# Loading beta in its final layout behind a weight load, and reordering two groups of casts, in an attention + MoE kernel

## The chip, the cores and the metric

The kernel runs on one core of one Trainium2 chip. The metric is device time in microseconds (us); a number given for a kernel is the median of its runs unless said otherwise. A profiled execution has in addition a span, which is about 1.7 us shorter than the time of the same execution (before: 283.81 us and 282.1 us). Names of engines: PE does matrix multiplies (its weight loads are listed apart as PEld), DVE is the vector engine, ACT the scalar engine, POOL is GpSimd, SP issues DMAs.

## The reference, cut to what matters

```python
# q, k, v: 8 batches x 8 heads x 576 x 64
q_s = exp(q - max) / sum            # softmax over the head dimension
k_s = exp(k - max) / sum            # softmax over the sequence
kv  = einsum("bhsd,bhse->bhde", k_s, v)
x   = einsum("bhsd,bhde->bhse", q_s, kv)      # -> 4608 tokens x 512
h   = x @ w_in                                # 512 x 2048
g   = h * (1 / (1 + exp(-beta * h)))          # beta: 2048 values
out = g @ w_out                               # 2048 x 512
```

## The kernel before

The parts that the change touches. `beta` (2048 floats) is loaded as four rows of 512, transposed on PE by four small matmuls, and multiplied by 0.5 into `beta_h`, which is the scale of every tanh.

```python
nc.gpsimd.dma_start(beta_r[:], moe_beta.rearrange("(b n) -> b n", b=4))
...
for blk in range(1, 4):                 # 512 columns of w_in each
    load_w_in(blk, 0, 2)                # SP; two rows of k-tiles per load
    load_w_in(blk, 2, 4)
for j0 in range(0, NJ, 2):
    load_w_out(j0)
make_identity(nc, ident[:])
make_identity(nc, identf[:])
...
dummy(4, CH)                            # warm-up matmuls
...
bt = bank("A1", [P, 4, 4], F32, "bt")
for i in range(4):
    nc.tensor.transpose(bt[:, i], beta_r[:, i:CH:4], identf[:])
dummy(1, CH)
...
nc.vector.tensor_scalar(beta_h[:], bt[:].rearrange("p i b -> p b i"), 0.5, None, op0=ALU.mult)
...
nc.scalar.activation(th[:], h[:], ACTF.Tanh, scale=beta_h[:, i // 4, i % 4 : i % 4 + 1])
```

Batch 0 is prepared at the head. While PE runs the MoE part of the first tokens, the loads of w_in, w_out and of batch 1's q, k and v arrive, and batch 1 is prepared in the same way (exp on ACT, sums and divisions on DVE, transposes and small matmuls on PE). From then on PE runs nearly without a gap.

The softmax here doesn't subtract the row's maximum and nothing guards it: scores larger than these inputs give would overflow.

## Time and profile before

| | before |
|---|---|
| time, median of 3 runs | 283.27 us (283.04 to 283.30) |
| span of the profiled run | 282.1 us |
| PE busy | 97% of the span |
| landing of q of batch 1, first half: median engine, last engine | 34.77 us, 36.88 us |
| first weight load of the dense part | 47.58 us |
| last weight load minus first of the dense part | 231.12 us |

"Landing" is read from the trace's completion records: each load has sixteen, one for each DMA engine, and an instruction that waits for the load waits for the last of them. The views of the profile that bound the time are shown in the prediction below. In the page's table of DMA queues of the kernel before (packets, MB, share of sixteen engines' span), these are the queues that bring instructions to the engines:

```profile
q8 instruction: 13, 0.21, 0.3%
q14 instruction: 10, 0.08, 0.1%
```

The trace has 16,384 bytes for each packet of the first and 8,192 for each of the second. And in the chain that ended last (start, length, what), the last piece is ACT's copy of the last output:

```profile
279.06 0.28 ACT o L532
```

The span ends at 282.07, so 3.01 us pass from the start of that copy to the end: the copy, the store, its landing, and the closing barrier.

### The profile page before, as it was taken

The numbers are of one execution on the slowest core, as the hardware profiler recorded it, in microseconds if no ns is written. First come the engines' busy times: TensorE is split into PE (matmuls) and PEld (weight loads), VectorE is DVE, ScalarE is ACT, GpSimd is POOL, SyncE is SP. The second block draws the span as 40 slices with busy tenths as digits, with TensorE's granted clock in tenths as the row PEclk, the third lists the DMA queues.
The fourth block names the chain that finished last, engine by engine and source line by source line (L and its number), as shares of the span: only waits on it lengthen the run. The fifth ranks groups of instructions, "written<-read, shape, count | busy, mean of one in ns | idle before, by whom it ended". The sixth has DMA issues, their size and how long they took to land.

```text
span 282.1 us, 4611 instructions
## 1 busy us (share of the span) xinstructions
PE 273.7 (97%) x1664; PEld 136.2 (48%) x1692; DVE 155.5 (55%) x282; ACT 168.1 (60%) x280; POOL 70.5 (25%) x120
## 2 busy tenths in 40 slices
PE   7989999999999999999999999999999999999995
PEld 3545445545444445444444444444444444444444
DVE  2947359976865485638564766466453333444401
ACT  4856367867965587457854785478454544444411
POOL 3368831450631054104510361027000000000000
PEclk9999999999999999999999999999999999999999
DMA  7999999889799908991699069904200200031112
GB/s 242 371 392 406 388 385 359 291 141 359 176 202 354 209 37 183 326 230 64 141 315 285 34 143 305 279 32 110 79 37 2 76 37 37 2 76 37 40 74 74
DMA packets 51559, 51.69 MB, mean 183 GB/s; under 512 B 21068, under 2 KB 41932, under 8 KB 51536
## 3 DMA queue, kind: packets, MB, share of 16 engines
q1 hardware_dynamic: 51360, 51.33, 60.9%
q8 instruction: 13, 0.21, 0.3%
q14 instruction: 10, 0.08, 0.1%
q10 hardware_dynamic: 144, 0.07, 0.1%
q0 software_dynamic: 32, 0.01, 0.0%
HBM read 38.28 MB, written 9.44 MB: 169 GB/s over the span
## 4 chain that ended last, share of the span: by engine, by line
PE 83%; DMA 13%; ACT 1%; issue 1%; SPq 1%; ACTq 0%
PE acc L509 40%; PE h L457 39%; DMA k<-in_k_dram 7%; DMA wo<-in_moe_w_out_dram 3%; DMA wi<-in_moe_w_in_dram 3%; PE kv L384 2%; PE x L408 2%; PE kv L259 0%; ACT Ek L230 0%; SPq L105 0%; ACT o L538 0%; SPq L117 0%; PE xt L422 0%; PE tp L217 0%; ACT va L152 0%
## 5 line engine op out<-in xcount | busy, mean ns | idle before, releaser
L471 DVE SCALAR_TENSOR_TENSOR g<-th,h 128x512 bf16<-128x512 bf16 x144 | 97.3, 685 | 98.5 <-ACT th L469 98.2
L469 ACT ACTIVATE th<-h,beta_h 128x512 bf16<-128x512 f32 x144 | 97.1, 689 | 85.7 <-PE h L457 82.7
L509 PE MATMUL acc<-w_out_b,g 128*128 128x512 bf16 (+2 forms) x590 | 142.8, 368 | 1.7 <-issue 1.1
L457 PE MATMUL h<-xT,w_in_b 128*128 128x512 bf16 x503 | 127.6, 379 | 1.0 <-POOL w_in_b L161 0.4
L457 PEld LDWEIGHTS <-w_in_b 128*128 128x128 bf16 x576 | 64.8, 113 | 61.9 <-POOL w_in_b L161 1.4
L509 PEld LDWEIGHTS <-g 128*128 128x128 bf16 x608 | 56.9, 98 | 63.9 <-issue 2.5
L315 POOL TENSOR_TENSOR Eq<-Eq,qz 128x512 bf16<-128x512 bf16 x24 | 25.1, 1049 | 84.3 <-issue 41.0
L538 ACT ACTIVATE o<-acc 128x512 f32<-128x512 f32 x34 | 20.0, 591 | 8.9 <-PE acc L509 7.4
L161 POOL TENSOR_SCALAR_AFFINE_SELECT va<-v 128x256 bf16<-128x256 f32 (+3 forms) x55 | 21.6, 427 | 13.8 <-DMA v<-in_v_dram 13.5
L355 ACT ACTIVATE Ek<-k 128x640 bf16<-128x640 f32 x24 | 17.7, 737 | 0.0
L457 PE MATMUL h<-xTt,w_in_b 128*128 128x512 bf16 x63 | 16.4, 379 | 0.1
L313 DVE TENSOR_REDUCE qz<-Eq 128x8 f32<-128x512 bf16 x24 | 16.2, 675 | 0.0
L305 ACT ACTIVATE Eq<-q 128x512 bf16<-128x512 f32 x24 | 14.7, 623 | 0.0
L201 DVE TENSOR_REDUCE qz<-Eq 128x16 f32<-128x1024 bf16 x4 | 4.9, 1216 | 10.8 <-ACT Eq L194 10.8
L166 DVE CAST xT<-x 128x512 bf16<-128x512 f32 x15 | 10.3, 685 | 0.6 <-PE x L408 0.5
L582 PE MATMUL warm<-zf 128*128 128x512 f32 (+1 forms) x14 | 9.0, 778 | 1.5 <-DVE zf L549 1.5
L161 POOL TENSOR_SCALAR_AFFINE_SELECT w_in_b<-wi 128x512 bf16<-128x512 f32 x16 | 9.5, 612 | 3.9 <-DMA wi<-in_moe_w_in_dram 3.8
L152 ACT CAST xT<-x 128x512 bf16<-128x512 f32 x17 | 9.7, 578 | 0.8 <-PE x L408 0.7
L194 ACT ACTIVATE Eq<-q 128x1024 bf16<-128x1024 f32 x4 | 4.2, 1056 | 9.5 <-DMA q<-in_q_dram 9.5
L341 POOL TENSOR_TENSOR Et<-Et,zt 128x512 bf16<-128x512 bf16 x4 | 4.2, 1042 | 21.0 <-DVE zt L340 21.0
L161 POOL TENSOR_SCALAR_AFFINE_SELECT w_out_b<-wo 128x1024 bf16<-128x1024 f32 x8 | 8.3, 1039 | 1.9 <-DMA wo<-in_moe_w_out_dram 1.8
L408 PE MATMUL x<-qT,kvn 64*64 64x512 bf16 x64 | 6.0, 391 | 0.4 <-ACT xT L152 0.4
(52 smaller groups left out, 78.3 us busy)
## 6 DMA issues: line engine op xcount, KB each, us to landing
q<-in_q_dram SPq DMA_DIRECT2D x16, 512.0 KB, 6.2
out_dram<-o SPq DMA_DIRECT2D x31, 256.0 KB, 3.1
k<-in_k_dram SPq DMA_DIRECT2D x24, 320.0 KB, 7.5
v<-in_v_dram SPq DMA_DIRECT2D x24, 320.0 KB, 7.5
wo<-in_moe_w_out_dram SPq DMA_DIRECT2D x8, 512.0 KB, 10.4
wi<-in_moe_w_in_dram SPq DMA_DIRECT2D x6, 512.0 KB, 9.7
k<-in_k_dram SPq DMA_DIRECT2D x4, 576.0 KB, 8.8
v<-in_v_dram SPq DMA_DIRECT2D x6, 288.0 KB, 8.6
```

The lines of the kernel that those rows point to most:

```text
L161: nc.gpsimd.affine_select(out=dst, in_=src, pattern=[[0, n]], base=0, channel_multiplier=0, compare_op=ALU.is_equal, fill=fill0,)
L166: eng.tensor_copy(dst, src)
L305: nc.scalar.activation(by_pair(Eq[b], m).rearrange("p t h d -> p h t d"), ld["q", b, hf][:, a : a + 2, :].rearrange("p h (t d) -> p h t d" ...
L313: nc.vector.tensor_reduce(z, e, axis=AX.X, op=ALU.add)
L315: nc.gpsimd.tensor_tensor(e, e, z.unsqueeze(3).to_broadcast((P, NT, 2, D)), ALU.mult)
L355: nc.scalar.activation(Ek[b][:, :, h0:h1, :].rearrange("p t h d -> p h t d"), ld["k", b, hf][:, a : a + h1 - h0, :].rearrange("p h (t d) - ...
L408: nc.tensor.matmul(xps[b, 2 * g + c][o, :], kvn[b][r, j, :], qT[b][r, g, a] if b < EARLY else qT[b][r, :, j, :], start=True, stop=True,)
L457: nc.tensor.matmul(hs[n, i][:], w_in_b[:, kt, blk * CH + r : (blk + 1) * CH : 4], rhs_a(n, kt), start=(kt == 0), stop=(kt == KT - 1),)
L469: nc.scalar.activation(th[:], h[:], ACTF.Tanh, scale=beta_h[:, i // 4, i % 4 : i % 4 + 1])
L471: nc.vector.scalar_tensor_tensor(out=g[:], in0=th[:], scalar=1.0, in1=h[:], op0=ALU.add, op1=ALU.mult)
L509: nc.tensor.matmul(acc[n, st][:, c0:c1], gs[n, j][:, min(st, 3) * P : (min(st, 3) + 1) * P], w_out_b[:, j, c0:c1], start=(j == 0), stop=(j ...
L538: nc.scalar.activation(o[:], acc[n, st][:], ACTF.Copy, scale=0.5)
```

## The change

The intent is to take beta's four transposes off PE and its copy off the path at the head, to have beta early enough for the first tanh all the same, and to take two places out where PE waited for a cast: w_in's second block (its second half now cast on POOL and DVE at once) and batch 1's v (ACT's part moved ahead).

```diff
@@ tiles
-    identf = const.tile([4, 4], F32, name="identf")
-    beta_r = const.tile([4, CH], F32, name="beta_r")
+    beta_p = const.tile([P, 4, 4], F32, name="beta_p")
@@ loads
-    nc.gpsimd.dma_start(beta_r[:], moe_beta.rearrange("(b n) -> b n", b=4))
     for blk in range(1, 4):
         load_w_in(blk, 0, 2)
+        if blk == 1:
+            nc.sync.dma_start(beta_p[:], moe_beta.rearrange("(b p i) -> p b i", b=4, i=4))
         load_w_in(blk, 2, 4)
     make_identity(nc, ident[:])
-    make_identity(nc, identf[:])
@@ head
-    bt = bank("A1", [P, 4, 4], F32, "bt")
-    for i in range(4):
-        nc.tensor.transpose(bt[:, i], beta_r[:, i:CH:4], identf[:])
-    nc.vector.tensor_scalar(
-        beta_h[:], bt[:].rearrange("p i b -> p b i"), 0.5, None, op0=ALU.mult
-    )
@@ behind x_out(0, 3)
+    nc.vector.tensor_scalar(beta_h[:], beta_p[:], 0.5, None, op0=ALU.mult)
@@ casts of w_in
-            cast_w_in(blk, k0, nc.gpsimd)
+            if (blk, k0) == (1, 2):
+                t, _ = ld["wi", 1, 2]
+                cast(nc.gpsimd, w_in_b[:, 2, CH : 2 * CH], t[:, 0])
+                cast(nc.vector, w_in_b[:, 3, CH : 2 * CH], t[:, 1])
+            else:
+                cast_w_in(blk, k0, nc.gpsimd)
@@ batch 1 (b_mm(n): n matmuls of the second MoE product put in between)
-        b_mm(20)
+        b_mm(6)
+        ev_cast(1, 0, 1, nc.scalar, 0, 4)
+        b_mm(14)
         ...
-        ev_cast(1, 0, 1, nc.scalar, 0, 4)
         ...
-        b_mm(1)
+        b_mm(2)
         ...
-        b_mm(4)
+        b_mm(3)
```

## The prediction

> **What bounds the kernel now.** I read the page first (PE busy 97% of a span of 282.1 us, so every microsecond gained or lost has to show as PE starting its dense part earlier or later), then the table by stage, then the chain of waits and the timeline of the first 48 us, because every line that the change touches runs there. The table by stage, with columns for length, PE, PEld, DVE, ACT and POOL busy time with counts, clock, DMA share and GB/s:
>
> ```profile
> 0.00:15.03 15.03, 12.74 (x96) 6.64 (x98) 8.63 (x20) 9.93 (x17) 5.43 (x19) 1.00 0.88 312
> 15.03:29.39 14.36, 13.92 (x62) 7.05 (x63) 8.81 (x15) 8.80 (x15) 10.54 (x17) 1.00 1.04 400
> 29.39:40.90 11.51, 11.34 (x52) 4.99 (x52) 4.95 (x8) 4.44 (x7) 6.02 (x7) 1.00 1.05 385
> 40.90:47.60 6.70, 6.32 (x72) 3.27 (x74) 6.03 (x15) 5.33 (x13) 1.95 (x4) 1.00 1.08 362
> 47.60:282.00 234.40, 229.36 (x1387) 114.25 (x1408) 127.04 (x228) 139.60 (x231) 46.61 (x76) 1.00 0.54 147
> ```
>
> The last stage, 234.4 us, is nearly pure matmul and the change does not touch it: its length is a constant, and the end moves by as much as its start, 47.6 us, moves. Up to 40 us the DMA engines are never idle (share 1.04, 1.05: saturated), and the chain of waits of that window says the same:
>
> ```profile
> 2.91 7.96 DMA k<-in_k_dram
> 10.89 8.77 DMA wi<-in_moe_w_in_dram
> 19.72 9.26 DMA wo<-in_moe_w_out_dram
> 28.99 10.90 DMA k<-in_k_dram
> 39.91 1.26 ACT Ek L230 x2
> ```
>
> The reader sees start and length: four loads cover 36.9 of the first 39.9 us. What then sets 47.6 is in the timeline of batch 1:
>
> ```profile
> 36.90 1.06 ACT L194 ACTIVATE Eq<-q 128x1024 bf16<-128x1024 f32 x1 [6.18 <-DMA q<-in_q_dram]
> 37.99 1.22 DVE L201 TENSOR_REDUCE qz<-Eq 128x16 f32<-128x1024 bf16 x1 [6.49 <-ACT Eq L194]
> ...
> 42.48 0.52 PEld L259 LDWEIGHTS <-Ek 64*128 64x128 bf16 x18 [0.82 <-ACT va L152]
> ...
> 43.49 0.45 PEld L217 LDWEIGHTS <-Eq 128*128 128x128 bf16 x8 [0.28 <-DVE Eq L205]
> ...
> 44.91 0.10 PEld L408 LDWEIGHTS <-kvn 64*64 64x64 bf16 x1 [0.43 <-DVE qT L166]
> 45.23 0.11 PEld L408 LDWEIGHTS <-kvn 64*64 64x64 bf16 x3 [0.22 <-ACT kvn L279]
> ...
> 47.16 0.20 PEld L408 LDWEIGHTS <-kvn 64*64 64x64 bf16 x4 [0.42 <-DVE kvn L281]
> ```
>
> ACT sat 6.18 us until q of batch 1 landed at 36.88. From there DVE works with hardly a gap (6.03 of 6.70 us in the stage): exp 1.06, reduce 1.22, reciprocal 0.25, multiply 1.23 end at 40.76, the second half's three end at 43.43, and PE's transposes at 40.91 and 43.49 start just behind them. The x matmuls at 45.23 wait for kvn on ACT, behind Ek at 42.92, which waits for k landing at 42.89. So four of the five waits shown hang on the landing of q or k of batch 1, and only the one at 42.48 on the order of the casts. From 36.88 to the first matmul of the dense part (47.58) I count 10.7 us of fixed chain.
>
> The completion records of the trace (sixteen for each load, one per DMA engine) show why these landings are late. The load of w_in block 1's second half lands on fifteen engines by 17.86 and on the sixteenth at 19.66; every later load keeps that gap (q of batch 1: 35.29 against 36.88). At 16.87 a 16,384-byte instruction packet of 1,095 ns went through one engine. One straggling engine sets the landing times.
>
> **What the Trainium skill says.** (1) "DMA: Bandwidth & Descriptors", section Specifications: below 512 bytes per descriptor a transfer does not reach line rate (a read-modify-write). The trace agrees: the loads of the q tails, 512 pieces of 256 bytes or 32 per engine, take 0.67 to 0.86 us between consecutive landings, 21 to 27 ns a piece, where 2,048 bytes take 84 ns. (2) Same page, "Issuing engines are not separate DMA queues": loads from POOL and SP share the same 16 engines. So moving beta to SP wins no bandwidth and puts it in line with the others. (3) "SBUF — State Buffer", section "Who interferes with whom": a DVE cast or tensor_scalar in a 2-port mode and a GpSimd instruction block each other for a whole instruction. The trace fits: DVE L289 took 0.50 us beside POOL's casts at 23.91 and 0.23 us at 53.25. (4) "Advanced Engine Details and Errata", ISA Cache: instructions come in lines of 16 KB, 256 instructions. The trace has 13 such packets; the first starts when PE has executed 217 instructions.
>
> **The change part by part.**
>
> Removed: the four transposes of beta. On PE they are 7.60 to 8.17:
>
> ```profile
> L597 PE MATMUL bt<-identf,beta_r 4*128 4x4 f32 x4 | 0.6, 262 | 0.0
> ```
>
> 0.57 us of PE time at the head. I give 0 of it to the end: the matmuls that follow wait elsewhere. kv of group 1 (12.39) follows POOL's cast of v, which follows v landing at 11.62; ACT's chain follows k landing at 10.87; x and then h at 15.03 follow these. DVE loses the beta_h multiply of 0.17 us at 12.12, but its next path instruction waits for kv anyway. POOL's identf (0.09 + 0.18 us) and beta's software DMA (0.70 us) go in front of an idle time of 5.9 us: 0.
>
> Added: one load of 512 pieces of 16 bytes, 32 per engine, on the saturated queue in front of w_in block 1's second half. Four-byte semaphore packets take 9 ns, 256-byte pieces 21 to 27 ns, most of it fixed (256 bytes at 2,048 bytes in 84 ns are 10.5 ns, so 11 to 16 ns are overhead). I estimate 9 to 16 ns for 16 bytes: 32 x 9 to 16 = 0.29 to 0.51 us, mid 0.4, on every engine including the straggler. Beta's old load, 2 KB on each of four engines, saves at most 0.08 us there. So every landing from w_in block 1's second half to v of batch 1 comes **0.35 us later**.
>
> Moved, cast of w_in: before, POOL cast k=2 and k=3 in turn from 19.72, and PE's first two matmuls on them ran at 20.39 and 20.95 where back-to-back spacing of 0.216 us would have had 20.21 and 20.43. With the landing at 20.0, if POOL and DVE overlap, both are cast by 20.7, and the second matmul starts at about 20.97: the move gains 0.34 and the landing takes 0.35, so PE comes out even. If they lock each other out (a DVE cast of some 0.35 to 0.6 us), PE comes out 0.3 later. DVE's own multiplies g wait behind that cast: g of unit 0 starts at about 20.4 instead of 18.54; at 0.62 us each, the eighth ends at about 25.9, just when PE wants its bank for unit 12. All this is before 29.39; PE then runs 52 matmuls and arrives at the transpose of batch 1 at 40.8 to 41.1, where Eq is not there before 40.76 + 0.35. So it is hidden either way.
>
> Beta's landing: 17.1 to 17.3 by my count (the load before it ends at 16.76 + 0.4), the multiply 0.17, and the first tanh needed it at 17.82: no wait, unless the instruction packet falls just on it. With eight PE instructions fewer ahead of it, that packet moves four matmuls (0.86 us) later, to about 17.7, past beta.
>
> Moved, cast of v: va comes from ACT at about 41.8 + 0.35 and from POOL at 41.9 + 0.35 instead of 42.43. PE's kv can start some 0.2 to 0.5 us earlier, but its result is first read by DVE (43.35), which is busy with Eq to 43.43 + 0.35. Hidden. The b_mm counts (one from the last group to the one before) only fill the gap so made.
>
> Sum: 0 (PE head) + 0 (casts, hidden) + 0.35 (landing of q and k of batch 1) = +0.35 us at 47.6 and at the end. 283.27 + 0.35 = **283.6 us**.
>
> **The rivals.** (a) *The removed work counts*: PE's 0.57 at the head, its 0.53 in stage two and 0.33 at 42.49 are all real, and if PE set the pace the end would come up to 1.4 us earlier, 281.9. PE's 97% and its near-gapless stages speak for it; against it, each of the gates after 40.9 names DVE or ACT, and those name DMA landings. (b) *The straggler changes*: the lag of 1.85 us after a packet of 1.1 us depends on what the engine is doing; behind other packets later in the trace I see lags from almost nothing to 1.7. A smaller lag by 0.7 would bring 282.9, one larger by 0.5 would bring 284.1. Nothing in this profile decides it, but the same loads surround the packet as before. (c) *Small pieces cost more than thought*: at 25 ns or more each, as the 256-byte pieces, 0.8 us, so 284.1. (d) *Beta comes late and ACT becomes the bound*: if the packet hits the straggler within beta's pieces, beta lands near 18.9 instead of 17.2; the tanhs start 1.2 us late, but POOL and DVE hold stage two back to about 20 anyway. I expect at most 0.3.
>
> **Range and chances.** Stage arithmetic gives +0.3 to +0.5 for my main reading; (b) and (c) stretch it to +0.9, and (a) or a smaller lag to −0.5. Runs of the kernel before differ by 0.26. I take 282.8 to 284.2. A change of 2% is 5.7 us, four times the most optimistic sum of what is removed, and no term on the other side is beyond 1.5: faster 0.01, within 2% 0.98, slower 0.01.
>
> **What would show each step.** Right: beta_p lands at 17.0 to 17.4; POOL's cast of block 1's k=2 starts at 20.0 to 20.2 (19.72 before); the exp of batch 1's q starts at 37.2 to 37.4 (36.90); the first transposes of batch 1 at 41.2 to 41.4 on PE with a wait for DVE's Eq longer than before; kv of batch 1 no longer behind ACT's va; dense part from 47.9 (47.58), 234.4 us long as before. Wrong: the exp of q no later than 36.9 (then the load is free, or the straggler moved); the dense part starting early although q is late (then PE or the casts were the gate); the last stage changing length by more than 0.2; PE waiting at unit 12 for a bank long enough to pass 41.2.

## The result

| | before | after |
|---|---|---|
| time, median of 4 runs each, side by side | 283.28 us (283.04 to 283.93) | 283.93 us (283.83 to 284.38) |
| span of the profiled run | 282.07 us | 282.14 us |

The ratio is 1.0022, with a 95% interval of 1.0002 to 1.0042. A ratio here is the mean time of one kernel's fast runs over the mean of the other's in the same rounds, so it is not quite the ratio of the medians.

The table by stage of the kernel after, with the same stretches and columns as in the prediction:

```profile
0.00:15.03 15.03, 11.41 (x88) 5.78 (x89) 8.17 (x18) 9.20 (x15) 5.36 (x15) 1.00 0.89 310
15.03:29.39 14.36, 14.10 (x68) 7.38 (x68) 9.64 (x18) 9.56 (x17) 10.80 (x16) 1.00 1.05 390
29.39:40.90 11.51, 11.51 (x58) 5.29 (x56) 5.31 (x8) 4.79 (x7) 6.01 (x7) 1.00 1.05 386
40.90:47.60 6.70, 6.46 (x74) 3.15 (x72) 6.03 (x16) 5.37 (x13) 1.69 (x4) 1.00 1.08 363
47.60:282.00 234.40, 231.10 (x1408) 114.12 (x1406) 126.82 (x227) 139.48 (x231) 46.73 (x76) 1.00 0.52 147
```

PE is busy for 11.41 us in the first stage in place of 12.74 (some 0.6 us of the difference are the four transposes; the stage is cut at a fixed time, and six matmuls more are counted in the next one), the DMA share is still above 1 from 15 to 47.6 us, and nothing became shorter: the first stages still end with a wait for loads. (A few matmul records were missing in the trace of before, hence 229.36 and 231.10 in the last line.) The chain that ended last says the same as before with other loads in it:

```profile
1.85 6.65 DMA k<-in_k_dram
8.52 7.18 DMA wi<-in_moe_w_in_dram
15.77 10.30 DMA wo<-in_moe_w_out_dram
26.15 10.46 DMA q<-in_q_dram
```

Four loads cover 34.6 of the first 36.6 us. The timeline of batch 1 after the change (start, length, engine, line, what; in brackets the idle time before it and what ended it):

```profile
36.63 1.06 ACT L193 ACTIVATE Eq<-q 128x1024 bf16<-128x1024 f32 x1 [5.82 <-DMA q<-in_q_dram]
...
41.89 0.52 PEld L258 LDWEIGHTS <-Ek 64*128 64x128 bf16 x18 [0.42 <-ACT va L151]
...
43.21 0.45 PEld L216 LDWEIGHTS <-Eq 128*128 128x128 bf16 x8 [0.59 <-DVE Eq L204]
...
44.63 0.10 PEld L407 LDWEIGHTS <-kvn 64*64 64x64 bf16 x1 [0.64 <-DVE qT L165]
...
46.89 0.20 PEld L407 LDWEIGHTS <-kvn 64*64 64x64 bf16 x4 [0.42 <-DVE kvn L280]
```

The moved cast of v did what it was for: PE's weight load of Ek comes at 41.89 in place of 42.48, that is 0.59 us earlier, of which 0.27 us come from an earlier landing of q (below) and 0.32 us from the cast. All the other lines moved only by as much as the exp of q: 36.90 to 36.63, 43.49 to 43.21, 47.16 to 46.89. The dense part starts at 47.31 in place of 47.58. In this execution q's last engine happened to land 0.27 us earlier (36.61 in place of 36.88), although its median engine landed 0.30 us later (35.07 in place of 34.77). The dense part is 231.11 us long, as before. So PE finished 0.27 us earlier, and yet the span is not shorter. The last piece of the chain, and the second instruction queue of the page's part on DMA queues:

```profile
278.78 0.28 ACT o L531
```

```profile
q14 instruction: 9, 0.07, 0.1%
```

From 278.78 to the end at 282.14 it is 3.36 us, where it was 3.01 us. And one instruction packet less is in the span. The experiments show that these two go together.

The w_in and beta part of the timeline after:

```profile
17.43 0.49 DVE L626 TENSOR_SCALAR beta_h<-beta_p 128x16 f32<-128x16 f32 x1 [0.97 <-DMA beta_p<-in_moe_beta_dram]
18.67 2.42 ACT L468 ACTIVATE th<-h,beta_h 128x512 bf16<-128x512 f32 x4 [2.34 <-PE h L456]
18.69 0.43 DVE L165 CAST w_in_b<-wi 128x512 bf16<-128x512 f32 x1 [0.77 <-DMA wi<-in_moe_w_in_dram]
18.73 0.86 POOL L160 TENSOR_SCALAR_AFFINE_SELECT w_in_b<-wi 128x512 bf16<-128x512 f32 x1 [0.27 <-DMA wi<-in_moe_w_in_dram]
```

Beta is there before the first tanh, which waits for PE. The DVE cast took 0.43 us and POOL's beside it 0.86 us, where POOL's casts of this size took 0.61 us alone.

### The profile page after: what moved, and what is told of

The parts are those of the page before. It is cut to its first block, busy times and chain, and to the rows that moved or that the text cites. A ratio compares the mean times of both kernels' runs of the same rounds, so it can differ in the third digit from the quotient of the medians.

```text
span 282.1 us, 4627 instructions
## 1 busy us (share of the span) xinstructions
PE 274.6 (97%) x1688; PEld 135.7 (48%) x1688; DVE 156.0 (55%) x283; ACT 168.4 (60%) x280; POOL 70.6 (25%) x116
## 4 chain that ended last, share of the span: by engine, by line
PE 83%; DMA 12%; DVE 2%; ACT 0%; SPq 0%; issue 0%; ACTq 0%; POOL 0%
PE acc L508 40%; PE h L456 39%; DMA q<-in_q_dram 4%; DMA wo<-in_moe_w_out_dram 4%; DMA wi<-in_moe_w_in_dram 3%; DMA k<-in_k_dram 2%; PE kv L383 2%; PE x L407 2%; DVE Eq L204 1%; DVE qz L200 1%; ACT Eq L193 0%; SPq L116 0%; PE xt L421 0%; DVE qT L165 0%; PE kv L258 0%
## 5 line engine op out<-in xcount | busy, mean ns | idle before, releaser
L508 PE MATMUL acc<-w_out_b,g 128*128 128x512 bf16 (+2 forms) x608 | 145.5, 368 | 0.0
L160 POOL TENSOR_SCALAR_AFFINE_SELECT va<-v 128x256 bf16<-128x256 f32 (+3 forms) x55 | 22.7, 450 | 13.8 <-DMA v<-in_v_dram 13.6
L354 ACT ACTIVATE Ek<-k 128x640 bf16<-128x640 f32 x24 | 17.7, 736 | 0.0
```

Of the source, the lines that this page charges most:

```text
L160: nc.gpsimd.affine_select(out=dst, in_=src, pattern=[[0, n]], base=0, channel_multiplier=0, compare_op=ALU.is_equal, fill=fill0,)
L354: nc.scalar.activation(Ek[b][:, :, h0:h1, :].rearrange("p t h d -> p h t d"), ld["k", b, hf][:, a : a + h1 - h0, :].rearrange("p h (t d) - ...
L508: nc.tensor.matmul(acc[n, st][:, c0:c1], gs[n, j][:, min(st, 3) * P : (min(st, 3) + 1) * P], w_out_b[:, j, c0:c1], start=(j == 0), stop=(j ...
```

## The experiments

Each of the twelve runs was timed beside the kernel before on the same chip; runs of one group share their rounds, and each group had another chip, so that across groups only the ratios to before can be compared. Four runs (e9 to e12) make up the third group, e5 to e8 the second, e1 to e4 the first. Before had medians of 283.40, 283.33 and 283.26 us in the three groups.

The theory to test: (A) the loads are the bound up to the landing of batch 1's q; beta's small pieces delay them; nothing of the work taken away counts. Rivals: (B) the difference is the run-to-run change of the engine that lands last; (C) the casts cost time. A fourth cause, the closing barrier, came up in the first profile of the kernel after. The expectations use letters of their own: in those of the first two groups, theory B is the closing barrier.

**e1, before unchanged.** No edit.

> The kernel before, unchanged, as a control for noise. All theories: ratio 1.000 within 0.001. Its profile is a second draw: if the straggling DMA engine is a fixed matter, w_in block 1's second half lands again about 1.8 us later on one engine than on the other fifteen and q of batch 1 lands at 36.9 within 0.1; if it is chance, the lag differs by 0.3 us or more, and q with it. Closing barrier: from GpSimd's first semaphore of the barrier to its second 0.08 us as in the first profile if that is fixed.

Measured: 283.31 us, ratio 0.9996 (0.9983 to 1.0009). Its profile has a span of 281.5 us, 0.6 us less than the first profile of the same kernel. q landed at 34.69 us on the median engine (34.77 in the first profile) but at 36.31 on the last (36.88), and the dense part started at 47.02 (47.58). So a single profile of the same kernel moves by 0.6 us, and all of that by the engine that lands last.

**e2, after unchanged.** No edit.

> The changed kernel, unchanged, timed closer. Theory A (beta's pieces delay the landing of q and k of batch 1, and these set the end): 0.1 to 0.4 us slower than before (ratio 1.0004 to 1.0014). Theory B (the end of the program, not the middle, got longer: GpSimd's two barrier semaphores 0.37 us apart instead of 0.08): about 0.3 us slower, and the 0.37 shows in this profile again. Theory C (the first profile's late first loads, k at 8.50 instead of 7.85, belong to the change): k of batch 0 lands at 8.4 or later again; if it is chance, near 7.9.

Measured: 284.12 us, ratio 1.0024 (1.0009 to 1.0039). The profiled run was the slowest, 285.50 us: q's last engine at 38.25 us, the dense part from 48.95 us. The increase of the first comparison is confirmed. The gap between GpSimd's two semaphore events in the closing barrier is 0.40 us (0.37 in the first profile of after); in before and e1 it is 0.08. The sign that this text gives for its theory C also came: k of batch 0 landed at 9.34 us. But it does not tell the change from chance, since e4 and e11, which load beta as before, have it at 8.54 and 8.75 us, and before and e1 at 7.86 and 8.16.

**e3, the beta part alone** (the before kernel with the change's hunks on tiles, loads, head and the new `beta_h` line; casts as before).

```diff
+            nc.sync.dma_start(beta_p[:], moe_beta.rearrange("(b p i) -> p b i", b=4, i=4))
-        nc.tensor.transpose(bt[:, i], beta_r[:, i:CH:4], identf[:])
```

> Only the beta half of the change: one load of 512 pieces, no transposes, no identf, casts as before. Theory A: as slow as the whole change (ratio 1.0004 to 1.0014), since the casts are off the path. Theory B: also as the whole change, if the missing software DMA or the shorter GpSimd program is what lengthens the barrier: 0.37 us there again. Rival (the casts' order is what costs): 1.000.

Measured: 283.52 us, ratio 1.0003 (0.9990 to 1.0016). Closing barrier: 0.09 us between the two events; so the missing software DMA, which this kernel lacks too, is not what lengthens it. q lands at 35.06 us on the median engine.

**e4, the casts alone** (the kernel after with beta's load and transposes as before).

```diff
-            cast_w_in(blk, k0, nc.gpsimd)
+            if (blk, k0) == (1, 2): ...            # one half on DVE
+        ev_cast(1, 0, 1, nc.scalar, 0, 4)          # between b_mm(6) and b_mm(14)
```

> Only the reordered casts, beta by transposes as before. Theory A: 1.000 within 0.0005, the kv of batch 1 starts 0.3 to 0.5 us earlier than 42.49, and the dense part still starts 10.7 us after q lands. Rival (casts were on the path): 0.998 to 0.999. Theory B: GpSimd's barrier semaphores 0.08 us apart as before.

Measured: 283.24 us, ratio 0.9994 (0.9981 to 1.0008). So the casts cost nothing and gain nothing that can be told from zero. Rival C falls. Closing barrier: 0.08 us.

Neither half alone shows the long barrier; the whole does. GpSimd executes 207 instructions in before, 203 in e3 and 206 in e4, and 202 in after: in the three kernels with 203 or more, an 8,192-byte packet comes at 193.8 to 198.0 us, and in after and e2 none comes there; one comes at 282.2 and 284.1 us instead, 0.06 and 0.31 us past the end of the span. So the barrier cannot have waited for that packet itself to land. My reading of this: GpSimd's instructions come in blocks, and the packet is sent for when it steps from one block into the next. In after, by this reading, that step falls between the two semaphore events of the closing barrier, where everything waits for it; with more instructions ahead of it, it falls at some 194 to 198 us, where GpSimd has nothing to do.

**e5, after with one GpSimd instruction more.**

```diff
     nc.gpsimd.memset(evens[:], 0.0)
+    nc.gpsimd.memset(evens[:], 0.0)
```

> The changed kernel with one more GpSimd instruction, a second memset of evens, early where GpSimd idles. Theory B in its present form: the changed kernel has 202 GpSimd instructions in its trace, one short of fetching its last 8 KB instruction packet during the loop (at 198.0 with 203 instructions, only at 282.2 and 284.1 with 202); the closing barrier waits for it. So here the packet comes near 198, the two barrier semaphores stand 0.08 us apart instead of 0.37 to 0.40, and the time falls by 0.30 us against the changed kernel, to a ratio of 1.0003 to 1.0014 against before. Rival (the barrier is longer because no software DMA ran, or the casts cost): nothing changes, 1.002 and more.

Measured: 283.66 us, ratio 1.0009 (0.9995 to 1.0022). The page's queue line and the last piece of the chain of e5:

```profile
q14 instruction: 10, 0.08, 0.1%
```

```profile
279.24 0.28 ACT o L531
```

The tenth packet is back (at 198.6 us), the gap between the events is 0.08 us, and with a span of 282.25 us the tail is 3.01 us again, as in before. An added instruction takes 0.35 us (3.36 to 3.01) off the end: 0.29 in that gap, the rest in the drain after it (0.08 us in place of 0.15). So the long barrier is shown to hang on GpSimd's instruction count: it stands in both profiles with 202 instructions and in none of the twelve with 203 or more. That the step between two blocks is what takes the time is the reading that fits, and was not tested further. In time, after and e2 had ratios of 1.0022 and 1.0024, e5 and its repeat e12 1.0009 and 1.0016: 0.2 to 0.4 us less, with intervals that overlap.

**e6, four loads of beta in place of one** (on e5), meant as four times the dose.

```diff
+            for x in range(3):
+                nc.sync.dma_start(
+                    beta_x[x][:], moe_beta.rearrange("(b p i) -> p b i", b=4, i=4))
```

> As the one with one more GpSimd instruction, and beta loaded four times in a row, three of them into tiles that nobody reads. Theory A: each load takes its share of every DMA engine; on the median engine the distance from the landing of w_in block 1's first half to that of its second half was 1.35 us without and 1.45 to 1.48 us with one load, so 1.8 to 2.0 us with four; q of batch 1 lands 0.35 to 0.5 us later on the median engine (35.4 to 35.6), and the time is 0.35 to 0.5 us above that with one load (ratio against before about 1.0015 to 1.003). Rival (such a load hides in gaps): the distance stays at 1.5 and the time at that of one load.

Measured: 287.97 us, ratio 1.0163 (1.0148 to 1.0177): 4.6 us above before and 4.3 us above e5, where 0.35 to 0.5 us above e5 was expected. The pieces are not what costs that. Read by the median engine, the four loads landed at 17.15, 17.33, 17.50 and 17.71 us, so 0.17 to 0.21 us each. What changed is when SP issues the loads behind them. SP's loads go through eight completion semaphores in rotation, and SP issues a load only when the load eight places before it has landed (in before, w_in's loads from the third to the tenth were issued 0.01 to 0.08 us after that landing). Four places went to 8 KB each. SP's issues in the timeline of e6, with single lines from narrower windows, and then of e5:

```profile
12.02 2.48 SPq L565 DMA_DIRECT2D beta_x<-in_moe_beta_dram  x3
14.54 5.41 SPq L139 DMA_DIRECT2D wi<-in_moe_w_in_dram  x5
```

```profile
13.43 1.07 SPq L565 DMA_DIRECT2D beta_x<-in_moe_beta_dram  x1
14.54 2.02 SPq L139 DMA_DIRECT2D wi<-in_moe_w_in_dram  x1
16.61 1.80 SPq L139 DMA_DIRECT2D wi<-in_moe_w_in_dram  x1
```

```profile
12.45 3.19 SPq L138 DMA_DIRECT2D wi<-in_moe_w_in_dram  x5
```

w_in's next load is issued at 14.54 in place of 12.45, and the DMA engines run dry. The places account for the first of the delays alone. The loads eight places before w_in's next four had landed at 14.08, 14.76, 15.44 and 17.11 us, and these four were issued at 14.54, 16.61, 18.52 and 19.02: SP was still at the issue before. An issue took 1.07 us for the last small load and 2.02 and 1.80 us for two of w_in's, where it took 0.37 or 0.38 us for each of these in e5. Why issues became so slow was not tested. The table by stage of e6 in steps of 2 us; the last two columns are the DMA share and GB/s:

```profile
14.00:16.00 2.00, 1.59 (x24) 0.81 (x17) 1.21 (x4) 1.65 (x4) 1.81 (x4) 1.00 1.07 375
16.00:18.00 2.00, 2.00 (x11) 1.04 (x10) 0.40 (x1) 0.00 (x0) 0.95 (x3) 1.00 0.82 108
18.00:20.00 2.00, 2.00 (x11) 1.08 (x10) 0.00 (x0) 1.81 (x3) 0.34 (x1) 1.00 0.72 212
20.00:22.00 2.00, 1.23 (x7) 0.45 (x6) 1.66 (x4) 0.58 (x2) 0.86 (x1) 1.00 0.68 223
```

In e5 the same three steps moved 347, 388 and 385 GB/s. The experiment failed as a measure of small pieces. It shows what three small loads more can set off at SP, places and slow issues together, and does not give the price of one place; the single load of beta in e5 takes a place too, and slows none of the issues just behind it. It also confirms the main chain from the other side: q's last engine lands 3.70 us later than in e5 (40.77 against 37.07), and the dense part starts 3.70 us later (51.47 against 47.77). Another 0.8 us is in the dense part, which takes 231.94 us here, with PE idle for 0.64 us until qT's load has landed, at 67.6 (see e7).

**e7, no load of beta at all** (on e5; a wrong scale, though the comparison with the reference still passed).

```diff
-            nc.sync.dma_start(beta_p[:], moe_beta.rearrange("(b p i) -> p b i", b=4, i=4))
-    nc.vector.tensor_scalar(beta_h[:], beta_p[:], 0.5, None, op0=ALU.mult)
+    nc.vector.memset(beta_h[:], 0.5)
```

> As the one with one more GpSimd instruction, but beta is not loaded at all: beta_h is set to 0.5 by a memset, so the result is wrong on purpose. No transposes and no load: what the removal alone is worth. Theory A: nothing, ratio 1.000 within 0.0007 of before, since the transposes were off the path; the median engine's distance of the two w_in landings is 1.35 us again. Rival (the removed transposes were on the path at the head): 0.998 or less.

Measured: 283.49 us, ratio 1.0002 (0.9990 to 1.0015), against 1.0009 for e5. Without transposes and without a load the kernel is not faster than before; the rival of this text (0.998 or less) falls.

**e8, beta loaded first, by ACT's queue** (on e5).

```diff
     nc.vector.memset(zf[:], 0.0)
+    nc.scalar.dma_start(beta_p[:], moe_beta.rearrange("(b p i) -> p b i", b=4, i=4))
```

> As the one with one more GpSimd instruction, with beta's load issued by ACT as the first thing of the program instead of by SP in the saturated stretch. Theory A: the DMA engines are not busy before 1.9 us, so the load costs less than in the stream: 0 to 0.15 us faster than with beta in the stream, not faster than the kernel before (1.000 to 1.0007). Rival: its pieces go in front of q of batch 0 and cost the same (1.0003 to 1.0014).

Measured: 283.76 us, ratio 1.0011 (0.9998 to 1.0023). The landings are as without beta: q at 34.88 us on the median engine (e7: 34.85), 36.38 on the last.

With these, the price of beta's load can be read without the noise of the last engine. From the first half of w_in's second block (the load ahead of beta) one goes back to the load before it and forward to the load behind beta, since loads overlap on the engines, and takes the difference of the two landings on the median engine:

| | w_in block 0, last part, to block 1, second half | q of batch 1, median engine |
|---|---|---|
| no beta between (before, e1, e4, e7, e8, e10, e11) | 2.70 to 2.75 us | 34.69 to 34.89 us |
| beta between (after, e2, e3, e5, e9, e12) | 3.00 to 3.05 us | 35.06 to 35.24 us |

The two groups don't overlap: 0.30 us, and it persists to q. That is the cost of one load of 512 pieces of 16 bytes on busy engines, some 9.5 ns for each of the 32 pieces of an engine (0.305 us / 32); in the trace of after the 512 packets of 16 bytes take 9 ns each. In e6, four such loads on end landed 0.17 to 0.21 us apart, so a further one added less. On the last engine, for which the kernel waits, the two groups overlap (q at 36.28 to 36.88 us without, 36.47 to 38.25 with), and in time this cost is not resolved: e5 over e7 and e9 over e10 are 0.0007 each (0.2 us), e5 over e8 is −0.0002, all inside the intervals.

But e7 and e8, with q early, did not end early: from the first weight load of the dense part to the last it was 231.62 and 231.64 us instead of 231.11. The timeline of e7 shows where:

```profile
63.06 0.63 PE L406 MATMUL x<-qT,kvn 64*64 64x512 bf16 x8 [0.44 <-DMA qT<-Eq]
```

PE waits for the transposing load of qT. It lands on fifteen engines at 61.44 us and on the sixteenth at 63.02, and a 16,384-byte instruction packet of PE started at 61.0 us, 4.2 us after that load was issued. In before, e1 and e4 this packet came 2.0 to 2.3 us after the issue, and the sixteenth engine was at most 0.1 us behind the median. The change removes eight PE instructions (four weight loads, four matmuls), which would put the packet there. The last group tests that.

**e9, e5 with eight PE instructions put back.**

```diff
     ev_cast(0, 0, 1, nc.gpsimd)
+    for _ in range(4):
+        nc.tensor.matmul(warm[:, 0:P], ident[:], ident[:], start=True, stop=True)
     dummy(1, CH)
```

> The kernel of e5 (changed kernel with one more GpSimd instruction) with four small matmuls put where the four transposes of beta were, so that PE's instruction count is again that of the kernel before (four weight loads and four matmuls more). Theory A (the third 16 KB instruction packet of PE, which comes 4.1 to 4.3 us after the issue of the transposing load of qT for want of these eight instructions, now and then holds up one of that load's sixteen engines by 1.6 us and PE's x matmuls at 63 us by 0.5 us): the packet comes 1.9 to 2.4 us after that issue again, the last engine of qT's load lies within 0.3 us of the median one, the dense part is 231.1 us from its first weight load to its last, and the time is 0.1 to 0.4 us below that of the repeat of e5 in the same rounds. Theory B (transposes of qT are held up by chance, not by that packet's place): packet anywhere, a stall at 63 us as likely as before. Theory C (the four transposes were on the path at the head): 0.3 to 0.6 us slower than the repeat of e5.

Measured: 283.68 us, ratio 1.0006 (0.9993 to 1.0020). The packet came 2.1 us after the issue; qT's last engine 0.07 us behind the median; dense part 231.11 us. Theory C of that text (the four transposes were on the path) falls as far as PE's time goes: with four matmuls back at their place the time did not rise. These four do not wait for beta, as the transposes did.

**e12, e5 unchanged again**, for the comparison with e9.

> e5 unchanged, for a comparison with e9 in the same rounds and a second profile. 283.5 to 283.8 us; the instruction packet of PE 4.1 to 4.3 us after the issue of qT's load; closing barrier with 0.08 us between GpSimd's two semaphore events. Theory A: a stall of about 0.5 us at 62.5 us with a chance of 3 in 7 (in the seven profiles with eight PE instructions fewer it was there in three).

Measured: 283.74 us, ratio 1.0016 (1.0003 to 1.0028). The packet came 4.2 us after the issue; no stall this time. The difference of 0.0010 to e9 (0.28 us) has the expected sign, but the intervals overlap.

**e10, e8 with the same eight PE instructions back.** The edits of e8 and e9 together.

> The kernel of e8 (beta loaded first, on ACT's queue, so nothing small between w_in's loads) with the same four small matmuls as e9. Every cost that was found is taken out: GpSimd's count keeps the closing barrier short, PE's count keeps the packet away from qT's load, and beta's load is not in front of w_in. Theory A: no stall at 63 us (there was one of 0.5 us in e8's profile), q of batch 1 lands at 36.3 to 36.9 us, dense part from 47.0 to 47.5 us and 231.1 us long, time 283.2 to 283.5 us, the same as the kernel before within 0.15 us and 0.2 to 0.5 below e8. Rival: the change gains its intended microsecond once its side costs are gone, 282.5 us or less.

Measured: 283.19 us, ratio 0.9999 (0.9986 to 1.0011). Packet 2.0 us after the issue, q's last engine at 36.33 us, dense part from 47.00 us and 231.12 us long, and no stall in the timeline:

```profile
62.45 0.63 PE L407 MATMUL x<-qT,kvn 64*64 64x512 bf16 x8
```

This is the change without its three side costs (and with four matmuls where the transposes were), and it is as fast as the kernel before, not faster. The rival of that text, a gain of a microsecond, falls.

**e11, before with eight PE instructions less.**

```diff
-    dummy(4, CH)
+    dummy(2, CH)
```

> The kernel before with two of its four first warm-up matmuls taken out (each is two weight loads and two matmuls, so eight PE instructions fewer, as in the changed kernel); beta and the casts as before. Theory A: the third instruction packet of PE moves from 2.0 to 2.3 us to 4.0 to 4.3 us after the issue of qT's load, in the middle of its pieces; with about 3 chances in 7 the last engine of that load is 1.6 us late and PE stalls 0.5 us at 63 us; the mean time rises by 0.0 to 0.4 us. Theory B: the packet stays where it was, no stall, same time. If PE's head mattered, the time would fall; I expect no fall.

Measured: 283.68 us, ratio 1.0012 (0.9998 to 1.0026). The packet moved to 4.1 us after the issue, in a kernel that is otherwise the one before. No stall in this profile (qT's last engine 0.25 us behind).

What follows from the last group: the place of the packet is set by PE's instruction count. That is shown in all fourteen profiles (2.0 to 2.3 us with the full count in before, e1, e4, e9, e10; 4.1 to 4.3 us with eight fewer in the other nine). That a packet at that place can hold up an engine of qT's load by 1.6 us, and PE by 0.4 to 0.6, is seen in e6, e7 and e8, in three of nine profiles, and in none of five with the packet at the other place. Three of nine against none of five may be chance. The trace shows that the place does change the load: its last engine is 0.16 to 1.67 us behind the median in the nine, 0.06 to 0.08 in the five. But the later place is no pure cost. From the issue to the last landing the load took 4.8 to 5.0 us in six of the nine, 6.2 to 6.4 in the three with a stall, and 5.2 to 5.5 in the five. Also in time, the three pairs that differ by these eight instructions have the same sign (e12 to e9, e8 to e10 and e11 to before: 0.0010, 0.0012 and 0.0012, so 0.3 us), but none of them alone is outside its interval, and e8 and e10 are of different groups. How much the packet costs on average stays open.

## Why the prediction was right, and where it was not

**The bound.** Right. In all fourteen profiles the dense part starts 10.67 to 10.71 us after q's last engine has landed, over a range of landings from 36.28 us (e4) to 40.77 us (e6). The 10.7 us of fixed chain that the prediction counted is the firmest number.

**Removed work is worth nothing.** Right. What shows it is the distance from q's landing to the dense part, 10.67 to 10.71 us with the transposes (before, e1, e4, e11) as without, and q's landing on the median engine, which is no earlier in e7 (34.85 us) than in before (34.77). The times agree: e7, with neither transposes nor load, is at 1.0002, though it had the stall at qT in its profile; e9, with four matmuls in place of the transposes, is not slower than e12; e11, with two warm-up matmuls less, did not get faster. (e10, at 0.9999, has matmuls put back, so it bears on the side costs and not on the removed work.) Their intervals would not show a gain below some 0.3 to 0.4 us.

**Beta's load.** Right in mechanism, and the size close: 0.35 us predicted at q's landing, 0.30 measured on the median engine; on the last engine, which sets the start, one execution does not show it. The term behind it was 9 to 16 ns a piece; 9.5 ns was measured, and the saving of 0.08 us for the old load was not visible: q landed at 34.69 to 34.89 us in before, e1, e4 and e11, which have the old load, and at 34.85 in e7, which has none.

**The landing times in the profile.** The single profile that was to show +0.35 showed −0.27, and the list of signs failed there: exp of q at 36.63 in place of 37.2 to 37.4, first transposes of batch 1 at 40.70 in place of 41.2 to 41.4, dense part from 47.31 in place of 47.9. An exp of q no later than 36.9 was one of the prediction's own signs of being wrong ("then the load is free, or the straggler moved"); the straggler had moved. The step that failed is "the same loads surround the packet as before", by which the straggling engine's lag was to stay. It changes from run to run of the same kernel: q's last engine was 2.11 us behind the median in the first profile of before and 1.62 in e1, and 1.54 in after and 3.10 in e2. Nor is the instruction packet its only source: in e9 one engine was 1.35 us behind the fifteenth already at the first landing of k (9.58 against 8.23 us), long before the packet at 18.58 us. So rival (b) was alive in each single execution. That it averages out over many is likely, since the landings on the median engine keep apart, but was not shown.

**The casts.** Hidden, as predicted; e4 alone is at 0.9994. The two engines did get in each other's way (POOL's cast 0.86 us in place of 0.61). POOL's cast started at 18.73 instead of 20.0 to 20.2, because the lag at that load was smaller in this execution. The moved cast of v brought PE's kv forward by 0.32 us (0.59 less the 0.27 by which q landed earlier), within the 0.2 to 0.5 predicted, but the prediction that kv would no longer stand behind ACT's va was wrong: the line still names ACT's va. It gained nothing, because the dense part waits for the chain behind q.

**Beta in time, and the packet.** Beta's last engine landed at 17.41 us (17.0 to 17.4 predicted) and the first tanh at 18.67 waited for PE. The first instruction packet came at 18.12 us (17.7 predicted).

**The end.** "The end moves by as much as its start" is the step that failed, by 0.35 us: in the pair of profiles the start moved by −0.27 and the end by +0.07. What was not in the prediction at all is the closing barrier, which became longer because GpSimd executes five instructions fewer. The dense part itself stayed at 231.11 us as predicted, in these two profiles; in e7 and e8 it grew by 0.5 us, and in e6 by 0.8, with the wait for qT, so it is not quite the constant that the prediction took it for.

**The sum.** The prediction had +0.35 us and 283.6; measured were +0.65 and 283.93. About 0.30 us is beta's load, about 0.35 us the closing barrier. This adds up to the measured increase, with PE's packet (0 to 0.3 us) left over and not resolved from the noise. But the interval of that increase reaches from 0.06 to 1.2 us, so that the close agreement may be luck; e3, which has beta's load and the moved packet, came out at only 1.0003. The prediction came near 283.93 although its sum lacks a term, the closing barrier, that is as large as the one it has. The gain of up to 1.4 us that the change looked for was off the path: it went into waits for the same loads.

## What to carry to other kernels

When loads set the start of the long stage, taking work off the engines ahead of it buys nothing, and a small load put among the large ones can delay all that land behind it (0.30 us for 512 pieces here). Several on end can also hold up the issue of the next large loads, which cost far more in e6 than the pieces did. To see a cost of 0.3 us, compare the landings on the median engine, not on the last one, and take several profiles. When an instruction count changes, look where the instruction packets went, at the end of the kernel as well.

## What the Trainium skill lacked or had wrong

- "Runtime: NRT & Kernel Launch", section "Instruction fetch mechanics", has every engine's instructions refilled in 16 KiB blocks and calls the cost of a block boundary "mostly hidden". PE's packets are 16,384 bytes here, but those of the second instruction queue are 8,192 bytes. And the cost is not hidden where the boundary seems to fall into the closing barrier (a reading that fits, not tested further): GpSimd's two semaphore events there are 0.37 to 0.40 us apart instead of 0.08, and one instruction more in the kernel (e5) takes the tail from 3.36 to 3.01 us.
- No page says that an instruction packet can delay one DMA engine of a load that is running: in e7, e8 and e6 the sixteenth engine of the transposing load came 1.6 us behind the median with such a packet in it. Three of nine profiles with the packet there showed it, and none of five with the packet two microseconds earlier; that the packet is the cause is not settled.
- "DMA: Bandwidth & Descriptors" has no figure for very small pieces on engines that are busy with other loads. Here one load of 512 pieces of 16 bytes cost 0.30 us, some 9.5 ns for each of an engine's 32 pieces; four such loads on end landed 0.17 to 0.21 us apart.
- No page gives the time that SP's issue of a large load can take when small loads are queued ahead of it: behind four loads of 8 KB two issues took 2.02 and 1.80 us in place of 0.37, and together with the places that the small loads took among the eight in flight this made the kernel 4.3 us slower than with one such load (e6 against e5).
